# Sixteen weight-spreading products at 112 columns instead of 28, with a zero product to open their bank

## The chip, the cores and the metric

The kernel runs on one core of one Trainium2 chip. Its time is the device time of one execution in microseconds (us); of several runs the median is taken. The engines of the core work side by side, each through its own queue in order: TensorE (PE in the profile, with its weight loads shown apart as PEld), VectorE (DVE), ScalarE (ACT), GpSimd (POOL) and SyncE (SP), which here issues nearly all DMA transfers. They wait for each other by semaphores.

## What is computed

A transformer block on 2048 rows of 448 features: a layer norm, a linear attention with 16 heads of 28 features, and a gated feed-forward part, each with its residual.

```python
def _A_ref(x, wqkv, w_phi, wo):
    qkv = (x @ wqkv).reshape(B, S, 3, H, Dh).transpose(2, 0, 3, 1, 4)
    q, k, v = qkv[0], qkv[1], qkv[2]
    pq = jnp.einsum("bhsd,hdf->bhsf", q, w_phi)
    pk = jnp.einsum("bhsd,hdf->bhsf", k, w_phi)
    phi_q = jnp.concatenate([_softmax(pq), _softmax(-pq)], axis=-1)
    phi_k = jnp.concatenate([_softmax(pk), _softmax(-pk)], axis=-1)
    kv = jnp.einsum("bhsf,bhsd->bhfd", phi_k, v)
    z  = jnp.einsum("bhsf->bhf", phi_k)
    num = jnp.einsum("bhqf,bhfd->bhqd", phi_q, kv)
    den = jnp.einsum("bhqf,bhf->bhq", phi_q, z)[..., None] + 1e-6
    o = num / den
    return o.transpose(0, 2, 1, 3).reshape(B, S, D) @ wo
...
x = A_x
h = x + _A_ref(_layernorm(x), A_wqkv, A_w_phi, A_wo)
g, u = _layernorm(h) @ w_gate, _layernorm(h) @ w_up
h2 = h + (sigmoid(g) * u) @ w_down
```

The part that the change touches is w_phi, the feature-map weights: 16 small matrices of 28 x 28, one for each head.

## The kernel before

All operations are written down by name in a graph, and the table ORDER gives for each engine the order in which they are issued; semaphores follow from which tiles an operation reads and writes. The waits of an operation stand ahead of its first instruction. Nothing is reordered at run time but for weight loads, which TensorE may start while an earlier product runs.

The 2048 rows lie in 16 tiles of 128. The stages are: loading x and the weights; layer norm statistics (L545, L546) on VectorE, the normalised tiles (L573, L576) and their transposes; folding w_phi into the key and query weights; the projections of keys, values and queries with the exponentials of the feature maps; the attention products; and the gated feed-forward part, which fills the last two thirds. From about 10 us on TensorE runs long chains of products through the helper at L311.

The folding is what the change belongs to. It computes, for each group of four heads, the product of the key weights with the feature-map weights, so that one projection gives the feature map directly. It needs w_phi as block-diagonal matrices `Wphi` (112 x 4 x 112: four groups, in each four blocks of 28 x 28). Three steps make them:

- `wph` is w_phi as it lies in memory, read as 112 rows of 112 numbers. Row r holds four consecutive rows of the small matrices, side by side in its 112 columns. It comes by a load issued from the scalar queue (the only one there).
- `wsp` (the function `spread`, L490) moves row 4*k+m's part into place on TensorE: for each group gg and each m from 0 to 3 a product whose weights are 112 columns of `zsel`, a matrix of zeros and ones made by POOL (L420), and whose streamed operand is the m-th 28 columns of `wph`. The four products of a group add up in 28 columns of PSUM bank 2; four groups fill 112 columns.
- `wex` (L494) on VectorE multiplies these with the mask `hmask`, repeating each group's 28 columns four times, and writes `Wphi`.

Around it on TensorE stand dummies (`warm0` to `warm9`, L524): products of a tile of zeros into bank 3, which nobody reads. The queue of TensorE begins so:

```python
"warm0 warm1 warm2 wsp warm3 wT0 wT1 warm4 wT2 wT3 warm5 w2m0_0 w2m0_1 w2m0_2 warm6 w2m0_3 xT1 xT0 warm7 "
"warm8 warm9 xT3 ppa0 ppb0 xT2 vva0 seed vvb0 ..."
```

`wT0` to `wT3` (L599) are transposes of the key weights `wk_sb`, four products each; `wTe0` to `wTe3` (L531) copy them to `WkT`, the second on VectorE and the others on ScalarE. `w2m0_*` (L612) are the products of `WkT` with `Wphi`, and `w2e0_*` (L531, "Wk<-psum") copy them to SBUF. `xT0` to `xT3` (L538) transpose normalised tiles of x, and `ppa0` is the first dense product. VectorE's queue begins `zero hmask mask2 bst1 bst0 agg1 agg0 wex wTe1 bst3 bst2 ...`, where `bst3` (L545) waits for the third load of x.

`warm0` is four dummies of 512 columns, `warm1` two of 512, `warm2` one of 128, `warm3` two of 128.

Of the kernel before, what the change touches and what calls it, by code (L numbers as in the profile page):

```python
# [18 lines left out]
class Graph:  # L19
# [9 lines left out]
    def op(self, eng, name, fn, r=(), w=(), dma=None, nring=0, after=(), rows=128, half=None, kb=0):  # L29
        o = _Op()  # L30
        o.engs = eng if isinstance(eng, tuple) else (eng,)
        fns = fn if isinstance(fn, tuple) else (fn,) * len(o.engs)
        k = o.engs.index(self.where[name]) if name in self.where else 0
        o.i, o.eng, o.name, o.fn, o.dma = len(self.ops), o.engs[k], name, fns[k], dma
        o.rows, o.half, o.kb = rows, half or {}, kb
        o.deps = {}
        r, w = self.flat(r), self.flat(w)
        o.need_inc, o.sem, o.val = False, None, 0

        def dep(j, raw):  # L40
            if j != o.i:
                o.deps[j] = o.deps.get(j, False) or raw
        for k in r:
            if k in self.lastw:
                dep(self.lastw[k], True)
        for k in w:
            if k in self.lastw:
                dep(self.lastw[k], True)
            for j in self.readers.get(k, ()):
                dep(j, False)  # L50
        for j in after:
            dep(j, False)
        if dma is not None and nring:
            lst = self.ring.setdefault(dma, [])
            if len(lst) >= nring:
                dep(lst[-nring], True)
            o.sem = (dma, len(lst) % nring)
            o.val = 16 * (len(lst) // nring + 1)
            lst.append(o.i)
        for k in w:  # L60
            self.lastw[k] = o.i
            self.readers[k] = []
        for k in r:
            if k not in w:
                self.readers.setdefault(k, []).append(o.i)
        self.ops.append(o)
        return o.i
# [131 lines left out]
DH = 28  # L199
G = 4  # L200
GP = 112
# [126 lines left out]
def build(nc, A_x, A_wqkv, A_w_phi, A_wo, B_w_gate, B_w_up, B_w_down, out):  # L328
# [10 lines left out]
    with ExitStack() as es:  # L339
        def sb(name, shape, d=dt.bfloat16):  # L340
            return es.enter_context(nc.sbuf_tensor(name, shape, d))
        f32 = dt.float32
        ident = sb("ident", [P, P])
        zero = sb("zero", [P, 512])
# [27 lines left out]
        wph = sb("wph", [GP, GP])  # L372
        zsel = sb("zsel", [GP, 452])
# [26 lines left out]
        def bk(i):  # L400
            return psum[:, i * 512:(i + 1) * 512]
# [6 lines left out]
        g = Graph()  # L408
        op = g.op

        def B(i):
            return ("bank", i)

        def load(name, dst, src, w, kb, r=(), eng="sp"):
# [7 lines left out]
           r=["zero"], w=["zsel"])  # L422
# [3 lines left out]
           r=["ident"], w=["ident"])  # L426
# [20 lines left out]
        def opads(e):  # L447
# [4 lines left out]
           w=[("phi", s) for s in range(NPHI)])  # L452
        op("pool", "wqpad", lambda e: e.memset(W2[1][:].rearrange("p k g n -> p (k g) n")[:, :, 56:64], 0.0),
           w=[("W2", 1, kt) for kt in range(KT)])
        op("dve", "mask2", lambda e: e.tensor_reduce(mask2[:], ident[:].rearrange("p (c h) -> p h c", h=2), AX.X, ALU.add),
           r=["ident"], w=["mask2"])
# [19 lines left out]
        def vload(k):  # L476
# [7 lines left out]
           r=["ident"], w=["hmask"])  # L484

        def spread(e):
            for gg in range(G):
                for m in range(4):
                    z = GP * gg - m + 3
                    p = e.matmul(bk(2)[:GP, gg * DH:(gg + 1) * DH], lhsT=zsel[:, z:z + GP], rhs=wph[:, m * DH:(m + 1) * DH],  # L490
                                 start=m == 0, stop=m == 3)
            return p
        op("pe", "wsp", spread, r=["zsel", "wph"], w=[B(2)])
        op("dve", "wex", lambda e: e.tensor_tensor(Wphi[:].rearrange("p g (l f) -> p g l f", f=DH),  # L494
                                                   bk(2)[:GP, 0:GP].rearrange("p (g f) -> p g f", f=DH)[:, :, None, :].to_broadcast([GP, G, 4, DH]),
                                                   hmask[:, None, :, None].to_broadcast([GP, G, 4, DH]), ALU.mult),
           r=[B(2), "hmask"], w=["Wphi"])
        vload(0)
# [22 lines left out]
        def warm(n, size):  # L521
            def f(e):
                for _ in range(n):
                    p = e.matmul(bk(3)[:, 0:size], lhsT=zero[:, 0:P], rhs=zero[:, 0:size], start=True, stop=True)  # L524
                return p
            return f
        for i, (n, size) in enumerate(((4, 512), (2, 512), (1, 128), (2, 128), (1, 128), (6, 128), (4, 128), (6, 128), (8, 128), (2, 128))):
            op("pe", "warm%d" % i, warm(n, size), r=["zero"], w=[B(3)])

        def evac(name, dst, src, rkey, wkey):  # L530
# [450 lines left out]
        at = {o.name: o.i for o in g.ops}  # L981
# [6 lines left out]
def bass_sequential_preLN__linear_kernel_hedgehog__glu_gated_glu__prompt_kernel(  # L988
    nc, A_x, A_wqkv, A_w_phi, A_wo, B_x, B_w_gate, B_w_up, B_w_down, out
):  # L990
    build(nc, A_x, A_wqkv, A_w_phi, A_wo, B_w_gate, B_w_up, B_w_down, out)
# [28 lines left out]
```

## Time and profile before

| what | value |
|---|---|
| median of 3 runs | 205.2 us (205.05, 205.20, 205.67) |
| span of the profiled execution, first to last instruction | 202.0 us |
| the profiled execution's own time beyond its span | not recorded apart; 205.2 - 202.0 = 3.2 us to the median |
| TensorE busy | 196.1 us, 97% of the span |
| VectorE busy | 132.2 us, 65% |
| ScalarE busy | 92.7 us, 46% |
| mean DMA rate | 81 GB/s |

The profile is one execution of the program. A row of its timeline has the start, the length, the engine, the line of the kernel, the operation and what it writes and reads, then how many instructions are merged into the row; in brackets stands the idle time of the engine ahead of the row and what ended it. A row of a line's own view has minimum, median and maximum of the duration in ns. The chain of waits follows the work that ended last back from the end.

Durations of single products are longer than the time from one to the next, since products overlap in the array; what a sequence of them takes is read from their starts.

### The profile page before, as it was taken

Reading aid. Unit: us, or ns where it says so; the run is one execution under the profiler, and the core shown is the slowest. Engines: PE = TensorE matmul, PEld = TensorE weight load, DVE = VectorE, ACT = ScalarE, POOL = GpSimd, SP = SyncE. Lnnn points to the kernel's source line nnn. Section 1 sums busy time; section 2 is a strip of 40 time slices with the busy share of each in tenths; the row PEclk is TensorE's granted clock in tenths of the full one; section 3 lists DMA queues with packets and bytes.
Section 4 is the critical chain, followed back from the end, with each engine's and each line's share of the span. In section 5 each row is a group of like instructions: output and inputs, shape, how many; then the busy total and the mean of one; then the engine's idle time right before and its main releaser. Section 6 shows DMA issues by size and latency. Waiting matters only on the chain.

```text
span 202.0 us, 5885 instructions
## 1 busy us (share of the span) xinstructions
PE 196.1 (97%) x2516; PEld 113.1 (56%) x2516; DVE 132.2 (65%) x319; ACT 92.7 (46%) x191; POOL 56.4 (28%) x95
## 2 busy tenths in 40 slices
PE   7899999999989999999999999999999999999995
PEld 4735656565558778676444444555555555554443
DVE  4899999978899677767758977436432422272224
ACT  3768998899772636222333342324422212222220
POOL 6579949533433613600041010001400000000000
PEclk9999999999999999999999999999999999999999
DMA  6955345849963320251005311030312000004003
GB/s 170 281 117 158 68 83 78 237 154 285 292 181 86 65 43 3 52 81 29 0 3 123 81 26 26 5 73 28 71 33 52 0 3 0 0 3 136 0 0 94
DMA packets 32491, 16.27 MB, mean 81 GB/s; under 512 B 24720, under 2 KB 31568, under 8 KB 32464
## 3 DMA queue, kind: packets, MB, share of 16 engines
q1 hardware_dynamic: 32336, 15.86, 32.0%
q8 instruction: 20, 0.33, 0.7%
q14 instruction: 7, 0.06, 0.1%
q10 hardware_dynamic: 128, 0.03, 0.1%
HBM read 8.34 MB, written 1.84 MB: 50 GB/s over the span
## 4 chain that ended last, share of the span: by engine, by line
PE 91%; DVE 4%; DMA 2%; SPq 1%; issue 1%; POOL 1%
PE psum L311 84%; PE psum L941 5%; DMA x_sb<-in_A_x_dram 2%; SPq L415 1%; DVE st L545 1%; PE psum L538 1%; DVE st L829 1%; POOL rst L833 1%; PE psum L612 0%; DVE hn_pad L851 0%; DVE xnT L531 0%; DVE b_sb L801 0%; DVE Wk L531 0%; DVE c_sb L804 0%; DVE rsm L798 0%
## 5 line engine op out<-in xcount | busy, mean ns | idle before, releaser
L311 PE MATMUL psum<-xnT,wg_sb 64*128 64x512 bf16 (+1 forms) x490 | 93.1, 333 | 0.2
L311 PE MATMUL psum<-xnT,wu_sb 64*128 64x512 bf16 (+1 forms) x490 | 92.9, 333 | 0.0
L913 ACT ACTIVATE sg_sb<-psum 128x512 bf16<-128x512 f32 (+1 forms) x70 | 34.8, 511 | 91.3 <-PE psum L311 90.8
L914 DVE SCALAR_TENSOR_TENSOR hhT<-sg_sb,psum 128x512 bf16<-128x512 bf16 (+1 forms) x70 | 38.9, 576 | 54.4 <-ACT sg_sb L913 54.2
L311 PEld LDWEIGHTS psum<-xnT,wg_sb 64*128 64x128 bf16 x490 | 44.4, 94 | 22.5 <-DVE hhT L914 4.2
L311 PEld LDWEIGHTS psum<-xnT,wu_sb 64*128 64x128 bf16 x490 | 44.4, 94 | 13.1
L311 PE MATMUL psum<-wd_sb,hhT 64*128 64x448 bf16 x336 | 36.9, 349 | 0.0
L311 PEld LDWEIGHTS psum<-wd_sb,hhT 64*128 64x128 bf16 x336 | 17.6, 94 | 14.5 <-DVE x_sb L836 0.5
L311 PE MATMUL psum<-Wk,xnT 64*128 64x448 bf16 x112 | 22.1, 350 | 0.2
L311 PE MATMUL psum<-wv_sb,xnT 64*128 64x448 bf16 x112 | 22.2, 351 | 0.1
L845 POOL TENSOR_SCALAR ve<-ssq 128x1 f32<-128x1 f32 x11 | 2.2, 200 | 55.0 <-ACT junk L842 54.8
L675 DVE TENSOR_REDUCE ss<-hhT 128x32 f32<-128x896 bf16 x16 | 16.6, 1054 | 0.3 <-ACT hhT L672 0.2
L721 ACT ACTIVATE eq<-psum 120x1024 bf16<-120x1024 f32 x16 | 15.7, 1024 | 1.0 <-PE psum L311 0.8
L685 POOL TENSOR_TENSOR phi<-hhT,rs 128x896 bf16<-128x896 bf16 x8 | 13.6, 1711 | 6.2 <-DVE rs L681 3.8
L311 PE MATMUL psum<-xnT,Wq 64*120 64x512 bf16 x112 | 15.0, 384 | 0.1
L810 POOL TENSOR_TENSOR o_pad<-c_sb,rden 128x448 bf16<-128x448 bf16 x10 | 9.3, 935 | 14.9 <-DVE rden L806 14.8
L311 PE MATMUL psum<-wo_o,oT 64*128 64x448 bf16 x56 | 13.2, 349 | 0.0
L311 PE MATMUL psum<-wo_e,oT 64*128 64x448 bf16 x56 | 13.1, 349 | 0.0
L941 PE MATMUL psum<-wd_sb,hhT 128*128 128x448 bf16 (+2 forms) x70 | 11.1, 315 | 0.0
L948 DVE SCALAR_TENSOR_TENSOR x_sb<-psum,x_sb 128x448 bf16<-128x448 f32 (+2 forms) x17 | 9.4, 592 | 2.7 <-PE psum L941 1.6
L311 PEld LDWEIGHTS psum<-Wk,xnT 64*128 64x128 bf16 x112 | 7.7, 94 | 5.6 <-PE psum L311 1.0
L801 DVE TENSOR_TENSOR b_sb<-psum,qq 128x464 bf16<-128x464 f32 x16 | 10.2, 637 | 0.7 <-PE psum L311 0.5
(103 smaller groups left out, 234.0 us busy)
## 6 DMA issues: line engine op xcount, KB each, us to landing
out_dram<-x_sb SPq DMA_DIRECT2D x15, 112.0 KB, 1.8
x_sb<-in_A_x_dram SPq DMA_DIRECT2D x7, 224.0 KB, 4.0
wd_sb<-in_B_w_down_dram SPq DMA_DIRECT2D x7, 224.0 KB, 4.0
wg_sb<-in_B_w_gate_dram SPq DMA_DIRECT2D x3, 448.0 KB, 6.3
wu_sb<-in_B_w_up_dram SPq DMA_DIRECT2D x3, 448.0 KB, 6.7
wv_sb<-in_A_wqkv_dram SPq DMA_DIRECT2D x2, 224.0 KB, 3.9
wk_sb<-in_A_wqkv_dram SPq DMA_DIRECT2D x2, 196.0 KB, 3.5
wo_e<-in_A_wo_dram SPq DMA_DIRECT2D x1, 336.0 KB, 3.1
```

Of the source, the lines that this page charges most:

```text
L311: p = e.matmul(o, lhsT=w, rhs=r, start=st, stop=sp, tile_position=(row, 0))
L415: return op(eng, name, lambda e: e.dma_start(dst, src), r=r, w=w, dma="in" if eng == "sp" else "ain", nring=48 if eng == "sp" else 8, kb=kb)
L675: op("dve", "ss%d" % t, lambda e: e.tensor_reduce(ss[:, s, :].rearrange("p (b h) -> p b h", h=2), eks.rearrange("p b (d h) -> p b h d", h= ...
L685: return e.tensor_tensor(phi[:, sp, :, :, :].rearrange("p b a n -> p (b a) n")[:, :, 0:56].rearrange("p b (d h) -> p b d h", h=2), eks.rea ...
L721: op("act", "eq%d_%d%s" % (c, i, "pm"[sg]), lambda e, sg=sg: e.activation(eq[c][:, sg, 2 * i:2 * i + 2, :].rearrange("p g n -> p (g n)"), ...
L801: op("dve", "b%d" % t, lambda e: e.tensor_tensor(h3(b_sb), OMv[:, :, :, 0:EV], h2(qq)[:, :, :, None].to_broadcast([P, NB, 8, EV]), ALU.mul ...
L810: return e.tensor_tensor(o_pad[:, t % NO, off:off + D].rearrange("p (h d) -> p h d", h=H), c_sb[:, t % NS, :, 0:DH], rden[:, t % NS, :][:, ...
L845: op(("pool", "dve"), "ve%d" % t, lambda e: e.tensor_scalar(ve2[:, t:t + 1], ssq2[:, t:t + 1], 1.0 / D ** 3, EPS, op0=ALU.mult, op1=ALU.ad ...
L913: op("act", "sig" + nm, lambda e: e.activation(sg_sb[:, k, 0:N], bk(bg)[:, 0:N], ACT.Tanh, scale=0.5), r=[B(bg)], w=[("sg", k)])
L914: op("dve", "hh" + nm, lambda e: e.scalar_tensor_tensor(out=hhT[(t0 // 4) % NHH][:, ff, ns], in0=sg_sb[:, k, 0:N], scalar=1.0, in1=bk(bu)[ ...
L941: p = e.matmul(bk(b)[:, lo:hi], lhsT=hb[:, ff, TS(t)], rhs=wd_sb[:, ff, lo:hi], start=ff == 0, stop=ff == FT - 1)
L948: op("dve", "fin%d%s" % (t, nm), lambda e: e.scalar_tensor_tensor(out=h_sb[:, t, lo:hi], in0=bk(b)[:, lo:hi], scalar=0.5, in1=h_sb[:, t, l ...
```

## The change

Each of the sixteen products of `spread` streams all 112 columns of `wph` instead of the 28 that are wanted, and puts them into bank 2 shifted by 28*m columns to the left, so that the m-th block of 28 lands on the first 28 columns of the group's own 112. The groups' fields are now 112 columns wide and begin at column 64. What lands beside a field's first 28 columns is not read, or lies in a field's other columns. One product (group 0, m = 3) would begin 20 columns ahead of the bank and is cut to 92 columns. Since the fields overlap, the products can no longer each open their own columns; a product of zeros over all 512 columns of the bank opens it, and all sixteen add to it. In exchange `warm1` has one dummy of 512 columns instead of two. `wex` reads the first 28 columns of each field, 112 apart.

```diff
         def spread(e):
+            e.matmul(bk(2)[:GP, :], lhsT=zero[:, 0:GP], rhs=zero[:, :], start=True, stop=False)
             for gg in range(G):
                 for m in range(4):
                     z = GP * gg - m + 3
-                    p = e.matmul(bk(2)[:GP, gg * DH:(gg + 1) * DH], lhsT=zsel[:, z:z + GP], rhs=wph[:, m * DH:(m + 1) * DH],
-                                 start=m == 0, stop=m == 3)
+                    at = 64 + GP * gg - m * DH
+                    lo = max(0, -at)
+                    p = e.matmul(bk(2)[:GP, at + lo:at + GP], lhsT=zsel[:, z:z + GP], rhs=wph[:, lo:GP], start=False, stop=gg == 3 and m == 3)
             return p
-        op("pe", "wsp", spread, r=["zsel", "wph"], w=[B(2)])
+        op("pe", "wsp", spread, r=["zero", "zsel", "wph"], w=[B(2)])
         op("dve", "wex", lambda e: e.tensor_tensor(Wphi[:].rearrange("p g (l f) -> p g l f", f=DH),
-                                                   bk(2)[:GP, 0:GP].rearrange("p (g f) -> p g f", f=DH)[:, :, None, :].to_broadcast([GP, G, 4, DH]),
+                                                   bk(2)[:GP, 64:64 + G * GP].rearrange("p (g x) -> p g x", x=GP)[:, :, None, 0:DH].to_broadcast([GP, G, 4, DH]),
                                                    hmask[:, None, :, None].to_broadcast([GP, G, 4, DH]), ALU.mult),
...
-        for i, (n, size) in enumerate(((4, 512), (2, 512), (1, 128), (2, 128), (1, 128), (6, 128), (4, 128), (6, 128), (8, 128), (2, 128))):
+        for i, (n, size) in enumerate(((4, 512), (1, 512), (1, 128), (2, 128), (1, 128), (6, 128), (4, 128), (6, 128), (8, 128), (2, 128))):
             op("pe", "warm%d" % i, warm(n, size), r=["zero"], w=[B(3)])
```

## The prediction, made before the changed kernel ran

> **What bounds the kernel now.** I read the page first, for the engine that is full, then the chain of waits, for what ends last in the first twelve microseconds, where the diff lies, and then the timeline of that stretch instruction by instruction.
>
> ```profile
> span 202.0 us, 5885 instructions
> PE 196.1 (97%) x2516; PEld 113.1 (56%) x2516; DVE 132.2 (65%) x319; ACT 92.7 (46%) x191; POOL 56.4 (28%) x95
> PEclk9999999999999999999999999999999999999999
> ```
>
> TensorE (PE) is busy for 97% of the span, so a microsecond that it loses once its dense work runs is a microsecond of the result. But the edit sits ahead of the dense work. There the chain of waits (start, length, what) reads:
>
> ```profile
> 2.60 4.05 DMA x_sb<-in_A_x_dram
> 6.65 0.02 issue
> 6.68 1.15 DVE st L545 x2
> 9.14 0.58 DVE Wk L531
> 9.72 0.07 issue
> 9.79 0.38 PE psum L538 x4
> 10.18 0.88 PE psum L311 x8
> 20.99 22.51 PE psum L311 x396
> ```
>
> Until 6.65 us the end is set by a load of x, which no product can hasten; from 6.68 VectorE (DVE) statistics and copies carry it, and from 10.18 TensorE does. Whatever happens on TensorE before 6.65 counts only if it is late enough to reach one of these pieces. The timeline (start, length, engine, line, then the idle time before and its releaser) of the edited stretch:
>
> ```profile
> 1.17 0.13 PEld L524 LDWEIGHTS psum<-zero 128*128 128x128 bf16 x2 [1.17 <-DVE zero L419]
> 1.57 0.15 PEld L524 LDWEIGHTS psum<-zero 128*128 128x128 bf16 x1 [0.28 <-issue]
> 2.85 0.15 PEld L524 LDWEIGHTS psum<-zero 128*128 128x128 bf16 x1 [0.28 <-issue]
> 3.28 0.15 PEld L524 LDWEIGHTS psum<-zero 128*128 128x128 bf16 x1 [0.28 <-issue]
> 3.71 1.10 PEld L490 LDWEIGHTS psum<-wph,zsel 112*112 112x112 bf16 x16 [0.28 <-issue]
> 3.81 1.10 PE L490 MATMUL psum<-wph,zsel 112*112 112x28 bf16 x16
> 4.71 0.15 PEld L524 LDWEIGHTS psum<-zero 128*128 128x128 bf16 x2
> 4.95 0.62 DVE L494 TENSOR_TENSOR Wphi<-psum,hmask 112x448 bf16<-112x448 f32 x1 [0.69 <-PE psum L490]
> 5.07 0.49 PEld L599 LDWEIGHTS psum<-ident,wk_sb 112*112 112x112 bf16 x8 [0.21 <-DMA wk_sb<-in_A_wqkv_dram]
> 5.07 0.62 PE L599 MATMUL psum<-ident,wk_sb 112*112 112x112 bf16 x8
> 5.72 0.39 DVE L531 COPY WkT<-psum 112x448 bf16<-112x448 bf16 x1 [0.15 <-PE psum L599]
> 5.79 0.49 PEld L599 LDWEIGHTS psum<-ident,wk_sb 112*112 112x112 bf16 x8 [0.22 <-DMA wk_sb<-in_A_wqkv_dram]
> 6.68 0.63 DVE L545 BATCH_NORM_STATS2 st<-x_sb 128x6 f32<-128x448 bf16 x1 [0.56 <-DMA x_sb<-in_A_x_dram]
> ```
>
> Two things are to be seen. The spread products (L490) are followed by idle time on both engines that use them: TensorE waits 0.21 for wk_sb before the transposes of L599, and again 0.22 before their second half; VectorE, after the expansion (L494) and one copy, waits 0.56 for x. And the tensor clock changes inside the products. The clock's row of the page has a 9 in its first slice too, so it does not record this; the durations do:
>
> ```profile
> L524 PEld LDWEIGHTS psum<-zero x36: 95/98/151, 1.2 to 9.3; 128*128 128x128 bf16 x36
> L490 PEld LDWEIGHTS psum<-wph,zsel x16: 132/132/218, 3.7 to 4.7; 112*112 112x112 bf16 x16
> 3.71 0.48 PEld L490 LDWEIGHTS psum<-wph,zsel 112*112 112x112 bf16 x4 [0.28 <-issue]
> ```
>
> The columns of the first two are minimum, median and maximum in ns; the third is the timeline cut at 3.70 to 4.09. Four of the sixteen loads start there; with the last between 0.13 and 0.22 long, (0.48 - 0.18)/3 = 0.10 us from one to the next. The other twelve fit between 4.09 and 4.71, 0.62/12 = 0.052 us apart. So the clock doubled at about 4.1 us; I call that the opening of the gate.
>
> **The change part by part.**
>
> *One dummy of 512 columns goes, a 512-column product of zeros comes.* Dummies start 0.427 us apart ((2.85 - 1.57)/3), so without one the 128-column dummy starts at 3.28, and by columns (0.427 x 128/512 = 0.107) TensorE is ready for the opening product at 3.39. It takes 0.427 and the first spread product starts at 3.81, as before. The count of products does not change. What moves is the wait: the op's waits (zsel from POOL, wph from its load) now stand ahead of the opener, at 3.39 instead of 3.71.
>
> ```profile
> 2.10 0.56 POOL L420 TENSOR_SCALAR_AFFINE_SELECT zsel<-zero 112x452 bf16<-112x452 bf16 x1
> 0.73 0.41 ACTq L415 DMA_DIRECT2D wph<-in_A_w_phi_dram  x1
> wph<-in_A_w_phi_dram ACTq DMA_DIRECT2D x1, 24.5 KB, 2.3
> ```
>
> zsel is ready at 2.66, wph at 0.73 + 2.3 = 3.03. Neither holds TensorE at 3.39; the margin falls from 0.68 to 0.36 us. Cost 0.00. No queue of another engine is touched: the same single load on the scalar queue, nothing on SP's or POOL's.
>
> *Sixteen products stream 112 columns instead of 28* (one of them 92). The nearest row is L599: same 112-column weights, 112 columns streamed, eight loads in 0.49 us, so (0.49 - 0.13)/7 = 0.051 us apart, the same as the 28-column products after the gate opened. The weight load sets the spacing, and streaming hides behind it. Before the gate the streamed columns would take 112 x 0.427/512 = 0.093 against the 0.10 measured. Lower bound: nothing; and a longer last product, by its tail of 84 columns, 84 x 0.427/512/2 = 0.035 us with the gate open. Upper bound: streaming isn't hidden at all and 84 columns are added to each, four at 0.070 and twelve at 0.035, 0.70 us. I take 0.04, since L599 has the very shape.
>
> *VectorE's expansion reads the bank at a stride of 112 columns instead of 28.* L494 still reads 448 elements with a broadcast and writes the same tile. No row shows another stride of this instruction; bounds are 0.62 (unchanged) and, from below or above, a tenth of it by the spread of BATCH_NORM_STATS2's durations over its own group:
>
> ```profile
> L545 DVE BATCH_NORM_STATS2 st<-x_sb x9: 582/609/628, 2.9 to 11.7; 128x6 f32<-128x448 bf16 x9
> ```
>
> That is (628 - 582)/609 = 8%, 0.05 us. I take 0.
>
> *Sum.* 0.00 + 0.04 + 0.00 = 0.04 us later for L494's end, 5.61 instead of 5.57. On VectorE only the copy at 5.72 follows before the 0.56 us of waiting for x, and that copy waits for L599, not for L494. The first product that reads Wphi (L612) starts at 6.58, 0.97 us later:
>
> ```profile
> 6.58 0.81 PE L612 MATMUL psum<-Wphi,WkT 112*128 112x112 bf16 x12
> 7.09 0.67 ACT L531 CAST Wk<-psum 128x448 bf16<-128x448 f32 x1
> 8.07 1.18 ACT L531 CAST Wk<-psum 128x448 bf16<-128x448 f32 x2
> 9.08 0.61 ACT L531 COPY xnT<-psum 128x512 bf16<-128x512 bf16 x1
> ```
>
> So nothing reaches the chain: 202.0 stays 202.0. If the cover were gone (x in time), the cost would be the 0.04 itself. The span is that of one execution; the median of the runs, 205.2, lies 3.2 us above it, for what runs around the span, and I carry that over: **205.2 us**. The three runs reach from 205.05 to 205.67, so what a measurement can tell from no change is about 0.3%, 0.6 us.
>
> **The rivals.**
>
> *A. The gate opens earlier, or more often early (faster).* While it is shut, a product of 28 columns keeps the array streaming for 28 x 0.427/512 = 0.023 of each 0.10 us; 112 columns keep it at 0.093. If what opens the gate is streaming, the products as they were are a hole of up to 16 x 0.10 = 1.6 us, and an execution whose decision falls inside or just behind it stays slow. Its price: with the gate shut the products are issued by 3.81 + 1.6 = 5.4 instead of 4.71, TensorE reaches the second half of the transposes at about 5.4 + 0.2 (two dummies) + 0.75 (eight at 0.094) + 0.1 (a dummy) = 6.45 instead of 5.79, is through them at 7.2 and through six dummies at 7.8. L612 then starts 1.2 us late. What TensorE can make up ahead of the dense products at 10.18 is the time that it was idle there:
>
> ```profile
> 8.00:9.00 1.00, 0.77 (x14) 0.73 (x14) 1.00 (x4) 1.00 (x3) 0.73 (x2) 1.00 1.40 133
> 9.00:10.00 1.00, 0.77 (x15) 0.62 (x11) 1.00 (x4) 0.69 (x2) 1.00 (x2) 1.00 1.13 271
> ```
>
> (The stretch, its length, then busy time of PE, PEld, DVE, ACT, POOL.) That is 2 x 0.23 = 0.46 us, and 1.2 - 0.46 = 0.74 is left, if the gate opens by then; ScalarE, 1.2 late at the cast of 7.09 and with 0.3 us to spare before the next (8.07 - 7.09 - 0.67), ends its copy at 9.69 + 0.9 = 10.6, 0.4 late. The longer route decides; I take 0.7. For it: 0.6 us is just the distance from the best to the worst run shown. Against it: the profiled execution opened at 4.1, where only four narrow products had run; two of three runs lie within 0.15 of each other at the low end, so the median may already be an early one. If the median execution is a late one, the change gives 205.2 - 0.7 = **204.5 us**.
>
> [...]
>
> *B. The wait at the opener (slower).* TensorE now stands still from 3.39 if wph lands later. Idle time itself is covered: up to about 0.5 us it is taken up by the waits for wk_sb and x. But idle time falls just ahead of 4.1, where the gate decided, and a gate that then stays shut costs A's price in the other direction. It decides from a landing more than 0.36 us later than the row shows, which is 16% more than its 2.3. For it: the loads of x in this stretch take from 2.1 to 4.6 us:
>
> ```profile
> DMA to landing us min/median/max: 2.1/4.0/4.6
> ```
>
> Against it: this one is issued first on its queue and is small. 205.2 + 0.7 = **205.9 us**.
>
> *C. Streaming is not hidden (hardly slower).* By the upper bound, 0.70 us, the expansion ends at 6.27 and its copy at 6.66, still ahead of the 6.68 at which x lets VectorE go on. TensorE comes 0.70 - 0.21 = 0.49 late to the first transposes, 0.49 - 0.22 = 0.27 late to the second, and the 0.46 us of idle time above swallow that. What is left is a chance that a cover runs short: 0 to 0.1, about **205.3 us**. Against it stands L599. [...]
>
> **How the numbers follow.** No change beyond the covered 0.04: 0.41. A: 0.36, since the rows show the gate and the edit's products at one place, and the spread of the runs is of A's size. B: 0.15. C: 0.08. Within 0.3% lie no change and C, less 0.02 for a cover that runs shorter than I found: 0.47. Faster by over 0.3%: 0.36, all of A. Slower: 0.15 + 0.02 = 0.17. The time is that of the likeliest, 205.2. Its own range is the runs' spread, 205.0 to 205.7. To leave out no more than 2 in 10 the range has to take in A, from 0.5 to a little over 0.74, and B: 204.3 to 205.9.
>
> **What would show it.** In the changed profile: the opener at 3.39 without an idle gap ahead of it, the first 112-column product at 3.81, sixteen loads 0.052 us apart once the gate is open, L494 at 4.95 to 5.0 and about 0.62 long, VectorE again idle 0.5 before the statistics at 6.68, ScalarE's cast at 7.1 and the dense products at 10.1 to 10.2. B would show as idle time before the opener released by wph, C as a spacing above 0.07 with the clock up. A would show as a clock that doubles earlier than 4.1, or, where the profile is alike, as runs that no longer reach the upper end of the spread. The prediction is wrong if the dense products start at the same time and the time still moves by more than 0.6 us, or if the opening of the gate lies elsewhere by more than a microsecond.

## The result, and the profile after

| | runs | median us | range us |
|---|---|---|---|
| before, measured beside it | 6 | 205.13 | 204.04 to 205.67 |
| changed | 6 | 204.02 | 203.73 to 204.32 |

The ratio is 0.9936, 95% interval 0.9913 to 0.9959: in these runs the changed kernel is 0.64% faster, about 1.1 to 1.3 us. 204.02 lies below the predicted range, on the side to which the prediction gave 0.36, while it held no change likelier.

The puzzle is in the profiles. The one of the changed kernel looks like the one of before (page; then the chain of waits; both with the columns of the prediction):

```profile
span 201.9 us, 5885 instructions
PE 196.3 (97%) x2516; PEld 114.0 (56%) x2516; DVE 132.3 (65%) x319; ACT 92.5 (46%) x191; POOL 56.5 (28%) x95
```

```profile
2.60 4.01 DMA x_sb<-in_A_x_dram
6.61 0.02 issue
6.63 1.15 DVE st L547 x2
...
9.10 0.58 DVE Wk L533
9.69 0.07 issue
9.75 0.38 PE psum L540 x4
10.14 0.88 PE psum L311 x8
```

Both spans agree within 0.1 us, both chains go through the load of x and VectorE, and the dense products begin at 10.14 and 10.18. By spans alone nothing was gained. But this profiled execution's own time is 203.73, 1.8 us above its span, and over the runs of all kernels below the time is 1.7 to 2.0 us above the span, nearly always 1.8 or 1.9. By an estimate from these, the execution profiled before, with its span of 202.0, took about 203.8 us. It was not like the median of 205.2. What lay between was hidden in the executions that weren't profiled.

The timeline of the changed kernel's start:

```profile
3.28 0.22 PEld L487 LDWEIGHTS psum<-zero 128*112 128x112 bf16 x1 [0.28 <-DMA wph<-in_A_w_phi_dram]
3.39 0.63 PE L487 MATMUL psum<-zero 128*112 128x512 bf16 x1
3.82 1.70 PE L493 MATMUL psum<-wph,zsel 112*112 112x112 bf16 x16
3.82 1.52 PEld L493 LDWEIGHTS psum<-wph,zsel 112*112 112x112 bf16 x15 [0.21 <-issue]
5.42 0.62 PEld L601 LDWEIGHTS psum<-ident,wk_sb 112*112 112x112 bf16 x8
5.55 0.62 DVE L496 TENSOR_TENSOR Wphi<-psum,hmask 112x448 bf16<-112x448 f32 x1 [1.23 <-PE psum L493]
6.01 0.50 PEld L601 LDWEIGHTS psum<-ident,wk_sb 112*112 112x112 bf16 x8
6.21 0.39 DVE L533 COPY WkT<-psum 112x448 bf16<-112x448 bf16 x1
6.63 1.15 DVE L547 BATCH_NORM_STATS2 st<-x_sb 128x6 f32<-128x448 bf16 x2
7.32 0.67 ACT L533 CAST Wk<-psum 128x448 bf16<-128x448 f32 x1
```

The opener starts at 3.39 and the first wide product at 3.82. All fifteen later loads are (1.52 - 0.21)/14 = 0.094 us apart (the last is taken as about 0.21 long), where the later twelve of the kernel before were 0.052 apart: by this spacing, from which alone I read the clock here and below, it is still at half throughout the products. It doubles within the first eight transposes (0.62 long, then 0.50). So in this execution the gate opened at about 5.6, 1.5 us later than in the profile of before, and it cost nothing, since x came at 6.61.

### The profile page after: what moved, and what is told of

It reads as the page before. It is cut to its first block, busy times and chain, and to the rows that moved or that the text cites. A ratio compares the mean times of both kernels' runs of the same rounds, so it can differ in the third digit from the quotient of the medians.

```text
span 201.9 us, 5885 instructions
## 1 busy us (share of the span) xinstructions
PE 196.3 (97%) x2516; PEld 114.0 (56%) x2516; DVE 132.3 (65%) x319; ACT 92.5 (46%) x191; POOL 56.5 (28%) x95
## 4 chain that ended last, share of the span: by engine, by line
PE 91%; DVE 4%; DMA 2%; SPq 1%; issue 1%; POOL 1%
PE psum L311 84%; PE psum L943 5%; DMA x_sb<-in_A_x_dram 2%; SPq L415 1%; DVE st L547 1%; PE psum L540 1%; DVE st L831 1%; POOL rst L835 1%; PE psum L614 0%; DVE hn_pad L853 0%; DVE xnT L533 0%; DVE b_sb L803 0%; DVE Wk L533 0%; DVE c_sb L806 0%; DVE rsm L800 0%
```

## The experiments

Each was timed in twelve executions beside the kernel before on the same chip, and one of the twelve was profiled. Put together, the 133 executions of the kernel before fall into two groups with a gap between: 55 from 203.26 to 204.27 (median 203.73) and 78 from 204.63 to 206.32 (median 205.47). The groups lie 1.74 us apart. For each experiment I give the median and how many of the twelve lie above 204.8, a mark that only two of the 78 miss. In brackets stand the ratio to the kernel before and its 95% interval.

**1. The kernel before, looked at again.** No edit.

> The kernel before, unchanged, for a second look at its gate. Theory (a hole in the streaming): most executions decide inside or behind the narrow products and stay at half clock until about 8 to 11 us; a profile of such an execution shows loads 0.09 to 0.10 us apart through the transposes and the folding products, the dense products starting 1.0 to 1.6 us after 10.1, a span near 203.3; the times fall into two groups, near 204.0 and near 205.1 to 205.7, the upper one the larger. Rival (the gate opens near 4 us in all executions and the change gained elsewhere): the profile again has its clock up at about 4 to 5 us whatever its time.

Median 203.92, four of twelve above 204.8; ratio 0.9973 (0.9934 to 1.0013) against the same kernel. The two groups are there, but in these twelve the lower was the larger, against what I expected; in the 35 executions run beside them 22 were in the upper one. The profiled execution was a lower one (204.0, span 202.1), so it shows no late gate: its sixteen loads take 1.24 us against 1.10 in the first profile, which puts the opening near 4.4. No upper execution of this kernel was profiled. A median of a dozen executions of this kernel is thus the outcome of a draw.

**2. The opener alone.** The products go back to 28 columns; opener, moved wait and the expansion's stride stay.

```diff
-                    lo = max(0, -at)
-                    p = e.matmul(bk(2)[:GP, at + lo:at + GP], ..., rhs=wph[:, lo:GP], start=False, ...)
+                    lo = m * DH
+                    p = e.matmul(bk(2)[:GP, at + lo:at + lo + DH], ..., rhs=wph[:, lo:lo + DH], start=False, ...)
```

> The changed kernel with the products back at 28 columns; opener, moved wait and the expansion's stride stay. Theory (the width counts): back to the time before, 205.1, a ratio to the kernel before of 0.998 to 1.002. Rival (the opener in place of a dummy, or the place of the wait, brings the gain): 204.0, ratio 0.994.

Median 205.36 (1.0018, 0.9986 to 1.0050), eleven of twelve above 204.8. The gain is gone, so opener, wait and stride don't bring it. This time the profiled execution is an upper one (205.52, span 203.6). Its timeline:

```profile
3.81 1.52 PEld L493 LDWEIGHTS psum<-wph,zsel 112*112 112x112 bf16 x15 [0.21 <-issue]
5.35 0.88 PEld L601 LDWEIGHTS psum<-ident,wk_sb 112*112 112x112 bf16 x8
6.20 0.88 PEld L601 LDWEIGHTS psum<-ident,wk_sb 112*112 112x112 bf16 x8
6.75 1.14 DVE L547 BATCH_NORM_STATS2 st<-x_sb 128x6 f32<-128x448 bf16 x2
7.59 1.19 PEld L614 LDWEIGHTS psum<-Wphi,WkT 112*128 112x128 bf16 x12
8.72 0.46 PEld L526 LDWEIGHTS psum<-zero 128*128 128x128 bf16 x4
9.52 0.63 PEld L540 LDWEIGHTS psum<-ident,xn_pad 128*128 128x128 bf16 x8
10.11 0.94 PEld L526 LDWEIGHTS psum<-zero 128*128 128x128 bf16 x16
```

The twelve folding products in the first profile of the kernel before:

```profile
6.53 0.70 PEld L612 LDWEIGHTS psum<-Wphi,WkT 112*128 112x128 bf16 x12
```

Eight transposes take 0.88 instead of 0.49, twelve folding products 1.19 instead of 0.70. The clock doubles within the eight transposes of x at 9.52 (0.63, where eight take 0.48 in profiles with the clock already up), so the gate opened near 9.8; the sixteen dummies behind them run at full clock, 0.94 as in the profile before. The chain of waits of the same execution:

```profile
1.17 2.42 PE psum L526 x6
3.60 0.43 PE psum L487
4.02 1.43 PE psum L493 x16
5.45 0.21 PE psum L526 x2
5.66 0.75 PE psum L601 x8
6.41 0.11 PE psum L526
6.51 0.75 PE psum L601 x8
7.26 0.64 PE psum L526 x6
7.90 1.12 PE psum L614 x12
9.02 0.43 PE psum L526 x4
9.45 0.37 PE psum L614 x4
9.82 0.52 PE psum L540 x8
...
10.53 0.78 POOL xn_pad L578
...
11.83 0.88 PE psum L311 x8
```

The load of x and VectorE's statistics have left the chain; these start at 6.75 without any wait for x. TensorE sets the end from the first dummy on, but for one normalised tile on POOL, and the dense products begin at 11.83 instead of 10.14: 1.69 us, against 1.7 between the two spans and 1.79 between the two times. That is the distance between the groups.

**3. and 4. Widths in between.** Products of 56 and of 84 columns:

```diff
-                    lo = max(0, -at)
+                    lo = min(m * DH, GP - 56)
```

(with the output cut to the same width; 84 in the other.)

> The changed kernel with products of 56 columns: while the gate is shut they stream half of the time. Theory: between the two, some executions late and some not, median 204.2 to 205.0. Rival (any width, the gain is the opener's): 204.0, all runs in one group.

> The changed kernel with products of 84 columns, which stream three quarters of the time while the gate is shut. Theory: the hole is nearly filled, 204.0 to 204.2, as the changed kernel. Rival (only back-to-back streaming counts): 205.1, as before.

With 56 columns the median is 203.91 (0.9956, 0.9923 to 0.9989) and three of twelve lie above 204.8, one of them, at 206.66, above both groups. My range for its median, from 204.2, was too high, since a median shows nothing of a minority. With 84 the median is 203.91 (0.9945, 0.9918 to 0.9972), the range 203.70 to 204.18, none above. By width, then: 28 columns eleven of twelve (the opener's kernel), 56 three, 84 none. Twelve executions each tell 28 from the other two; they don't tell 56 from 84.

**5. The changed kernel, twice more.**

> The changed kernel, unchanged, beside the next two. Theory (the gate opens after a stretch of dense streaming, and only the narrow products broke it): every run in the lower group, 203.7 to 204.4, ratio to before 0.993 to 0.996. Rival (it only shifts the odds for one chip or moment): some runs at 204.9 to 205.9.

> The changed kernel beside these: 203.5 to 204.4, median 203.9.

Medians 203.87 (0.9967, 0.9935 to 0.9998) and 203.72 (0.9955, 0.9926 to 0.9983). With the first six that is thirty executions from 203.44 to 204.72, none of them above 204.8, where the kernel before has 76 of 133.

**6. The opener ahead of the wait**, in place of the last 512-column and the 128-column dummy.

```diff
-"warm0 warm1 warm2 wsp warm3 ..."
+"warm0 wopen wsp warm3 ..."
```

> The opener stands ahead of the wait for wph, and the 512-column and the 128-column dummy ahead of it are gone: the first wide product at about 3.29 instead of 3.82. Theory: streaming stays dense, so no late group; where the gate opens between 5 and 7 the products and transposes end up to 0.5 us earlier, so the upper end falls to about 204.0 and the median to 203.7 to 203.9. Rival (what counts is the number of dummies ahead of the products): some runs late, 205 and more.

Median 203.75 (0.9959, 0.9929 to 0.9988), 203.35 to 204.52, none above 204.8. The products start at 3.28. Beside the changed kernel of the same chip and hour (203.87) that is no difference that I can tell; the upper end did not fall to 204.0 as I expected.

**7. Narrow dummies, first try.** The wide products stay; the five 512-column dummies become twenty of 28 columns.

```diff
-... (4, 512), (1, 512), (1, 128), (2, 128), ...
+... (16, 28), (4, 28), (1, 128), (2, 128), ...
```

> The wide products stay, but the first five dummies of 512 columns become twenty of 28 columns, 0.107 us apart by their weight loads while the gate is shut: as long on TensorE, as many weight loads and more products, a quarter of the streaming. Theory (streaming columns count): the dense stretch begins at 3.3 instead of 1.2, the gate opens 2.1 us later, between 6.0 and 9.4, and half or more of the runs lie above 204.5, median 204.5 to 205.3. Rival (products or weight loads count, however narrow): as the changed kernel, 204.0.

Median 204.94 (1.0022, 0.9993 to 1.0051), range 204.41 to 205.60, six of twelve above 204.8 and none in the lower group: the gain is gone. But the run doesn't tell the theories apart, since my premise failed:

```profile
1.17 0.64 PEld L526 LDWEIGHTS psum<-zero 128*128 128x128 bf16 x21 [1.17 <-DVE zero L419]
3.11 0.17 PEld L487 LDWEIGHTS psum<-zero 128*112 128x112 bf16 x1 [1.30 <-DMA wph<-in_A_w_phi_dram]
```

Twenty-one loads of 128 columns take 0.64 us, 0.03 apart, where those of 112 columns follow 0.094 apart. TensorE then stood idle for 1.30.

**8. Narrow dummies without idle time.** Twenty-three of 28 columns with weights of 112 columns.

```diff
+                    m = GP if size == DH else P
-                    p = e.matmul(bk(3)[:, 0:size], lhsT=zero[:, 0:P], rhs=zero[:, 0:size], start=True, stop=True)
+                    p = e.matmul(bk(3)[:m, 0:size], lhsT=zero[:, 0:m], rhs=zero[:, 0:size], start=True, stop=True)
...
-... (4, 512), (1, 512), (1, 128), (2, 128), ...
+... (18, 28), (5, 28), (1, 128), (2, 128), ...
```

> The wide products stay, but the first five dummies of 512 columns become twenty-three of 28 columns with weights of 112 columns, whose loads were 0.094 us apart while the gate was shut: no idle time (the twenty of 28 columns with 128-column weights went 0.03 apart and left TensorE idle from 1.8 to 3.1). Loads and products run without a pause, only the streaming is thin. Theory (streaming columns count): the gate opens late, after 6, all or nearly all runs above 204.3, median 204.5 to 205.3. Rival (a busy TensorE counts, however thin its streaming; the run before was late for its idle time): 203.5 to 204.4, median 203.9.

Median 205.98 (1.0053, 1.0023 to 1.0084), all twelve at 205.1 or above.

```profile
1.17 2.25 PEld L527 LDWEIGHTS psum<-zero 128*112 128x112 bf16 x24 [1.17 <-DVE zero L419]
3.40 0.64 PE L487 MATMUL psum<-zero 128*112 128x512 bf16 x1
3.83 1.70 PE L493 MATMUL psum<-wph,zsel 112*112 112x112 bf16 x16
6.29 0.88 PEld L602 LDWEIGHTS psum<-ident,wk_sb 112*112 112x112 bf16 x8
7.67 0.78 PEld L615 LDWEIGHTS psum<-Wphi,WkT 112*128 112x128 bf16 x12
10.93 1.74 PE L311 MATMUL psum<-Wk,xnT 64*128 64x448 bf16 x14
```

TensorE is never idle ahead of the opener, which starts at 3.40 as in the changed kernel, and the wide products follow. Only the streaming of the first 2.2 us is thin (28 columns for each load, 0.094 us apart), and the gate opens near 7.9 (twelve folding products in 0.78, between the 0.70 of the kernel before and the 1.19 of experiment 2), where it opened near 5.6 in the first profile of the changed kernel. That all twelve are late agrees with streaming, not occupation, as what counts; but the time is more than that explains: the dense products are 0.9 us late in this profile, while its time, 206.11, is 2.4 above the changed kernel's. The rest arises later, and its cause stays open (the chain of waits passes a 4.57 us transpose transfer at 62.55 and VectorE at 95 to 97, where the changed kernel's does not).

**9. to 11. Another way to close the hole.** If loads of 128 columns go 0.03 us apart, sixteen narrow products with the selection matrix cut 128 wide would pass in 0.5 us (`zsel` is made 468 columns wide for it). All else is as before the change. The second leaves out one 512-column and the 128-column dummy ahead of the products, the third has seven dummies behind them instead of two.

```diff
-p = e.matmul(bk(2)[:GP, gg * DH:(gg + 1) * DH], lhsT=zsel[:, z:z + GP], ...
+p = e.matmul(bk(2)[:, gg * DH:(gg + 1) * DH], lhsT=zsel[:, z:z + P], ...
```

> The kernel before with one edit: the narrow products take 128 columns of the selection matrix as weights instead of 112, since 128-column loads went 0.03 us apart with the gate shut. Sixteen products take 0.5 us instead of 1.5, streaming 0.023 of each 0.03. Theory: the hole is gone with no wider product and no opener: no late group, 203.3 to 204.2, median 203.6 to 203.8, at or below the changed kernel. Rival (28 columns are too few whatever their spacing): as the kernel before, two groups, median 205.1.

> The same, with one 512-column and the 128-column dummy ahead of it left out, so that the products begin at 3.3 instead of 3.8. Theory: median 203.4 to 203.7, if the half microsecond counts where the gate opens after 5; the same as the run before if x's load covers it. Rival (fewer dummies lose the gate): a late group again.

> The narrow products with 128-column weights again (in that run 3 of 12 executions were late, TensorE idle 0.18 before the key weights landed), now with seven 128-column dummies behind them instead of two, so that TensorE streams until the key weights land at about 5.1. Theory (thin streaming and idle time add up to the hole): no late group or at most one run in twelve, median 203.5 to 203.9, all but one below 204.5. Rival (narrow products are themselves too thin, whatever follows): three or more of twelve above 204.8.

The first: median 203.99 (0.9972, 0.9935 to 1.0009), three of twelve above 204.8, though I expected none. The second, begun half a microsecond earlier, has a median of 204.94 (0.9992, 0.9960 to 1.0025) and eight of twelve. I had overlooked what waits next:

```profile
3.28 0.64 PE L490 MATMUL psum<-wph,zsel 112*128 112x28 bf16 x16
5.09 0.82 PEld L600 LDWEIGHTS psum<-ident,wk_sb 112*112 112x112 bf16 x8 [1.23 <-DMA wk_sb<-in_A_wqkv_dram]
11.12 0.38 PE L539 MATMUL psum<-ident,xn_pad 128*128 128x128 bf16 x4 [0.23 <-POOL xn_pad L577]
```

The products are through at 3.9, and TensorE idles 1.23 us for the key weights: the hole is back as idle time. There are also two dummies fewer ahead; experiment 6 leaves out the same two with wide products and has none above 204.8. The third fills it with five more 128-column dummies:

```profile
3.81 0.64 PE L490 MATMUL psum<-wph,zsel 112*128 112x28 bf16 x16
4.27 0.67 PEld L524 LDWEIGHTS psum<-zero 128*128 128x128 bf16 x7
4.89 0.88 PEld L599 LDWEIGHTS psum<-ident,wk_sb 112*112 112x112 bf16 x8
```

Median 203.83 (0.9941, 0.9909 to 0.9974), 203.45 to 204.35, none of twelve above 204.8. A kernel with 28-column products and no opener thus does what the change does, when they are packed closely and TensorE streams on behind them. It is no faster than the changed kernel. How much the five dummies add to the first of the three, with its three of twelve, twelve executions can't tell.

**The profiles together.** The opening is read from the spacing of the loads. In six profiles (the kernel before and the changed one, experiments 1 and 6, the first and the third of 9 to 11) it lies between 4.1 and about 6.9 us; the weight loads of the dense products then begin at 9.8 to 10.3, and the executions took 203.5 to 204.4 us (the first one by the estimate above). In four it lies near 7.9 (experiment 8), 8.8 (7), 9.5 (the second of 9 to 11) and 9.8 (2); there they begin at 10.9 to 11.8, and the executions took 205.2 to 206.1. So an opening up to about 7 us cost next to nothing here, and a later one moved the dense products.

## Why the prediction was wrong

**The direct costs were right.** The opener and the first wide product came out as worked out (3.39 and 3.82, against 3.39 and 3.81), without idle time beyond the 0.28 that stood ahead of each earlier load; wph held nothing up. Streaming 112 columns is hidden behind the weight load while the clock is at half: fifteen loads take 1.52 us, as with 28 columns in experiment 2. The expansion took 0.62 at either stride. It started at 5.55, not at the 4.95 to 5.0 forecast, because the clock stayed at half through the products, not because they were wider (with 28 columns it started at 5.48 in experiment 2); x, which came at 6.61, covered that. So sixteen such products at full clock, the 0.04 of the sum, weren't seen in this profile. Rivals B and C did not happen in it.

**The step that failed is the last of the sum**: "the median of the runs, 205.2, lies 3.2 us above it, for what runs around the span, and I carry that over". What lies around the span is 1.8 us. The other 1.4 showed that the profiled execution was not a median one but one of the lower group, and that the chain of waits on which I built "no change" does not hold for the majority. In the upper execution of experiment 2 TensorE itself is the chain from 1.17 us on, and the 0.56 us of cover on VectorE is not there. That the upper executions of the kernel before look the same is inferred from the equal distance between the groups.

**Rival A is the one that the runs agree with, and two of its arguments misled.** "Two of three runs lie within 0.15 of each other at the low end, so the median may already be an early one" took 205.05 and 205.20 for the low end; they belong to the upper group, and 204.04 came with the next three runs. And its price of 0.7 us was too small by a factor of two and a half: I let the gate open by the folding products (L612, about 7.5 to 8); in experiment 2 it stayed shut to 9.8, so the folding products (twelve in 1.19 us instead of 0.70), their dummies (four in 0.46 instead of 0.26) and the first transposes of x (eight in 0.63 instead of 0.48) ran at half clock too, and the groups lie 1.74 us apart. The change takes away the upper group; with 78 of 133 executions in it, that is 0.59 x 1.74 = 1.0 us in the mean. The means of all executions, 133 before and thirty changed, differ by 0.82: the thirty have a median of 203.91, 0.18 above that of the lower group, and what makes this isn't shown. That the first medians lie 1.1 apart owes something to the luck of the draw, since five of those six executions before were upper ones.

**That the hole keeps the gate shut** is shown as far as runs from outside can show it. The cleanest pair is experiment 2 against the changed kernel, with the same instructions and TensorE occupied in both and only the streamed width different: eleven of twelve against none of thirty, and none of twelve with 84 columns on the same chip as experiment 2. Experiment 8 (thin streaming earlier) and the second of 9 to 11 (idle time) also have late executions; wider products, or narrow ones packed closely and followed by dummies, take them away. Why the gate opens early in one execution and late in another is not shown: with narrow products it opened near 4.1 and near 4.4 in two executions of the kernel before and, with the opener, near 9.8 in a third. The products' hole lasts up to 1.5 us (fifteen loads in 1.52); where the gate opened near 4.1, only the 0.4 us from 3.71 on stood ahead of the opening, and near 9.8 the whole hole did. Nor does a run show how much streaming is enough: 56 columns still left three late of twelve, 84 none, and that is all there is on it.

**My own marks for being wrong.** The dense products started at the same time in both profiles and the time moved by 1.1 us, as the last sentence named; the other mark, the opening of the gate more than a microsecond elsewhere, also came (5.6 for 4.1), in an execution that lost nothing by it. One profile per kernel could not have decided between no change and A; the list of times could.

## What to carry to other kernels

Compare the profiled execution's own time with the median before building on its chain of waits: where the median lies further above the span than a profiled execution's own time does, the profile shows another kind of execution than the median one. While the spacing of the loads shows the tensor clock still at half, try to keep TensorE streaming wide operands without a break until it doubles: here sixteen products of 28 columns, spread out by weight loads 0.094 us apart, left eleven of twelve executions late (experiment 2), much like 1.23 us of idle time with eight of twelve (the second of 9 to 11), and products of 112 columns, whose loads took the same 1.52 us, left none of thirty. Where a short stage ahead is sped up, look at what is then waited for: in the second of 9 to 11 the half microsecond gained came back as 1.23 us of idle time, with eight late of twelve against three, a difference that so few executions don't settle.

## What was not expected of the hardware

Before the clock doubled, loads of 128 columns for products of 28 followed each other in 0.03 us (twenty-one in 0.64, experiment 7), those of 112 columns in 0.094 (fifteen in 1.52, experiment 2); sixteen products of 28 columns took 0.64 us with the former (the first of 9 to 11) and 1.63 with the latter (experiment 2). And the profile's own row for the granted clock has a 9, its highest digit, in every slice of both kernels' profiles, and the mean granted clock is 1.0 also in the execution whose loads ran at half pace to 9.8 us (experiment 2): what changed there was read from the spacing of the loads alone.
